# The sigmoid of the decay taken as a tangent, with its halving on GpSimd

## The chip, the cores and the metric

The kernel runs on one core of a Trainium2 chip. The metric is the device time of one execution in microseconds, the median of several runs. A core has TensorE (matmuls), VectorE, ScalarE (activation functions from a table, and copies), GpSimd and SyncE (which issues most of the transfers). In profiles they are PE, DVE, ACT, POOL and SP; PEld is TensorE's loading of weights.

## The reference

Two stages in a row. The first is a gated linear recurrence over 768 tokens for 4 batches and 8 heads of size 48; the second an MLP with a gelu over all 3072 tokens (384 to 2048 to 384).

```python
def _attn_ref(q, k, v, f_logit):                     # (4, 8, 768, 48) each
    f = 1.0 / (1.0 + np.exp(-f_logit))
    state = np.zeros((B, H, D, D))
    for t in range(S):
        state = f[:, :, t, :, None] * state + np.einsum('bhd,bhe->bhde', k[:, :, t], v[:, :, t])
        y[:, :, t] = np.einsum('bhd,bhde->bhe', q[:, :, t], state)

def _moe_ref(x, w_in, w_out):                        # x: y as (3072, 384)
    h = x @ w_in
    g = h * (1.0 / (1.0 + np.exp(-1.702 * h)))
    return g @ w_out
```

## The kernel before

The work is cut into 12 units of 256 tokens, numbered n, three to a batch. A unit n goes through an attention part and, later, its MLP.

Attention treats a unit as four chunks of 64 tokens. F holds the decay f of a unit as 128 x 1024 numbers in one buffer, since four pairs of heads times 256 tokens lie along it. From F, GpSimd makes products of neighbours over 1, 2, 4, ... 32 tokens (`begin_gates`, L383, tile tot, one buffer that is reused from unit to unit). With F and then with these products VectorE scales the keys and queries in X, level by level (`promote`, L473 in units 0 to 2 and L477 later). Ahead of each such step ScalarE sets the keys aside (Kc, L448, and Qc, L454), and TensorE takes the scores (sc, L392), which VectorE masks into A (L421, L441). The values v are summed by A (y, L488); the state st is carried over the chunks on VectorE (L594, L595), and adds its share to y (L616). ScalarE copies y to yT (L627), and transfers turn yT into xT, the input of the MLP.

The MLP multiplies xT by w_in (h, L785), applies the gelu on ScalarE (g, L789, the function Gelu_apprx_sigmoid), and multiplies g by w_out (o, L811 in blocks for units 0 to 2, L762 later, where seven products take the place of eight). The weights come in as 32-bit words, and are converted once, in units 0 to 4, by one ScalarE instruction (L217, tile a) and four of VectorE (L219 to L222).

How F comes about differs by unit. In units 0 to 2 (`n < N_FILL`, N_FILL is 3) TensorE transposes the raw logits (L344) into PSUM, and ScalarE evicts them with four activations of 128 x 256 (L349); in units 0 and 1 the function of this eviction is the sigmoid, in unit 2 it is a copy, and the sigmoid follows in one instruction on all of F (L355). From unit 3 on VectorE transposes the raw logits into F in two halves (L332), and one activation of 128 x 1024 applies the sigmoid in place (L337).

ScalarE takes its functions from a table that is loaded in sets; where the next function is not in the set that is loaded, the compiler puts a load ahead of it (ACT_TABLE_LOAD in the profile, at the line of the function that it is for). The sigmoid and the gelu lie in different sets.

The order on TensorE is written out by hand, and for units 0 to 3 that of all engines: `merge` runs through the parts of a unit's attention and puts matmuls of the MLP between them, with pieces of the weight conversion on VectorE and ScalarE. The parts that prepare unit n + 1 (`begin_f`, `begin`, `begin_k`, `begin_gates`) are placed among those of unit n. PSUM tiles for h, o and the transposes share one tag "mm" of four buffers, so TensorE cannot start the next h before ScalarE has emptied one of them.

Of the kernel before, what the change touches and what calls it, by code (L numbers as in the profile page):

```python
# [12 lines left out]
AF = mybir.ActivationFunctionType  # L13
ALU = mybir.AluOpType


def view(t, offset, dims):

    a = t[:]
    return bass.AP(a.tensor, a.offset + offset, [list(a.ap[0])] + [list(d) for d in dims])  # L20
# [3 lines left out]
def kernel(  # L24
# [33 lines left out]
    nc = tc.nc  # L58
# [18 lines left out]
    N_FILL = 3  # L77
    HALF = U // 2
    SLOT = NP * HALF
# [68 lines left out]
    F = const.tile([P, NA], F32, name="F")  # L148
# [21 lines left out]
    for r in range(NGR):  # L170
        ffs = range(r * FG, (r + 1) * FG)
        for ff in ffs[::2]:
            f = slice(ff * P, (ff + 2) * P)
# [65 lines left out]
    def load_raw(n, j, engines=(nc.sync,)):  # L239
        if n >= NALL:  # L240
            return
        b, s0 = n // NU, n % NU * U
        src = (f_logit, q, k)[j]
        first = s0 - (j == 1)

        def span(head, token, dims, d=0):
            return bass.AP(src.tensor, src.offset + ((b * H + head) * S + token) * D + d, dims)
        if n < N_FILL:
            for a in range(NP):
                engine = engines[a * len(engines) // NP]  # L250
                to = by_pair[j][32 * a:32 * (a + 1), :, :R * D]
                if first < 0 and a == 0:

                    for r, rows in ((1, 16), (17, 15)):
                        engine.dma_start(
                            out=to[r:r + rows], in_=span(0, r * R - 1, [[R * D, rows], [S * D, 2], [1, R * D]])
                        )
                    engine.dma_start(out=to[:1, :, D:], in_=span(0, 0, [[R * D, 1], [S * D, 2], [1, (R - 1) * D]]))
                else:
                    engine.dma_start(out=to, in_=span(2 * a, first, [[R * D, 32], [S * D, 2], [1, R * D]]))  # L260
            return
        for f in (1, 0):
            for r in range(4):
                lo = 32 * (r % 2)
                width = R4 * D - lo
                part = span(r // 2, first + (0 if f else HALF), [[R4 * D, 32], [2 * S * D, NP], [1, width]], lo)
                nc.sync.dma_start(out=by_half[32 * r:32 * (r + 1), j, f, :, :width], in_=part)
            if f and first < 0:
                for r in range(4):
                    lo = 32 * (r % 2)  # L270
                    nc.sync.dma_start(
                        out=by_half[32 * r:32 * r + 1, j, f, :, :D - lo],
                        in_=q[b - 1, r // 2::2, S - 1:S, lo:].rearrange("a t d -> t a d"),
                    )
# [31 lines left out]
    def attention(n):  # L306
# [8 lines left out]
        ORDER = (1, 0) if n % 2 == 0 else (0, 1)  # L315
# [10 lines left out]
        def turn(j, outs, fn=None):  # L326

            if n >= N_FILL:
                for f in (1, 0):
                    out = outs(f)  # L330
                    at, step = (0, 1) if f else (HALF - 1, -1)
                    nc.vector.transpose(  # L332
                        view(out, at, [[HALF, NP], [step, R4], [R4 * step, 32]]),
                        by_half[:, j, f].rearrange("p a (j d) -> p (a j) d", j=R4)[:, :, :32],
                    )
                if fn:
                    nc.scalar.activation(F, F, fn)  # L337
                return
            for j0 in range(0, R, 4):
                pt = ps.tile([P, 4, P], F32, tag="mm", name=f"t_{n}_{j}_{j0}", bufs=4)  # L340
                for jj in range(4):
                    for h in range(2):
                        x = (j0 + jj) * D
                        nc.tensor.matmul(  # L344
                            pt[h * HS:(h + 1) * HS, jj, :], lhsT=by_pair[j][:, h, x:x + HS], rhs=ident, start=True, stop=True
                        )
                for f in (1, 0):
                    at, step = (j0, 1) if f else (HALF - 1 - j0, -1)
                    nc.scalar.activation(  # L349
                        view(outs(f), at, [[HALF, NP], [R * step, 16], [step, 4]]),  # L350
                        pt.rearrange("p j (a f i) -> p f a i j", a=NP, f=2)[:, 1 - f],
                        fn if fn and n < N_FILL - 1 else AF.Copy,
                    )
            if fn and n == N_FILL - 1:
                nc.scalar.activation(F, F, fn)  # L355

        def begin_f():
            turn(0, lambda f: F[:, ORDER.index(f) * SLOT:(ORDER.index(f) + 1) * SLOT], AF.Sigmoid)
            if n >= N_FILL or (n == 1 and 0 == 0):
                load_raw(n + 1, 0)  # L360

        def begin():
            turn(1, lambda f: slot(query(n, f)))
            if n >= N_FILL or (n == 1 and 1 == 0):
                load_raw(n + 1, 1)

        def begin_k():
            turn(2, lambda f: slot((KR, KF)[f]))
            if n >= N_FILL or (n == 1 and 2 == 0):
                load_raw(n + 1, 2)  # L370
            if n >= N_FILL:
                set_aside(0, True)
                promote(0)
            else:
                set_aside(0)
# [268 lines left out]
        def to_x(y, x, ng):  # L644

            queue = nc.sync if n else nc.scalar
            for h in range(2):
# [3 lines left out]
                while at < D:  # L651
# [5 lines left out]
                    at += w  # L657

        return (begin_f, begin, begin_k, begin_gates), parts


# [353 lines left out]
```

## Time and profile before

Three runs took 627.27, 628.38 and 629.58 us; the median is 628.38 us. The profiled execution has a span of 627.9 us.

| engine | busy us | share of the span | instructions |
|---|---|---|---|
| TensorE, matmuls | 602.8 | 96% | 7314 |
| TensorE, weight loads | 517.5 | 82% | 7314 |
| VectorE | 385.8 | 61% | 632 |
| ScalarE | 260.3 | 41% | 544 |
| GpSimd | 39.9 | 6% | 91 |

The weight loads overlap the matmuls. ScalarE's busy time holds 20 table loads. In a line of the timeline the first number is the start in us, the second the length, then come engine, source line, operation, output and inputs, and in brackets the idle time before it with what ended it. In a line of the groups the numbers after the bar are the group's busy time in us, the mean of one instruction in ns, and the idle time ahead of it.

### The profile page before, as it was taken

What the parts mean: (1) busy time and instruction counts of PE and PEld (TensorE: products, weight loads), DVE (VectorE), ACT (ScalarE), POOL (GpSimd) and SP (SyncE); (2) the same over time, 40 slices, a digit from 0 to 9 for tenths busy, and PEclk for the clock granted to TensorE, in tenths of its full rate; (3) what the DMA queues carried; (4) which work ended last, traced back from release to release, by engine and by line L of the source; (5) the groups of instructions that cost most, each with busy time, mean ns of one, the idle gap of its engine ahead of it and who ended that gap; (6) DMA issues with size and microseconds to landing.
All of it is one profiled execution on the core that took longest, in us unless ns stands there. A gap on an engine that the chain in (4) does not pass through costs nothing.

```text
span 627.9 us, 17094 instructions
## 1 busy us (share of the span) xinstructions
PE 602.8 (96%) x7314; PEld 517.5 (82%) x7314; DVE 385.8 (61%) x632; ACT 260.3 (41%) x544; POOL 39.9 (6%) x91
## 2 busy tenths in 40 slices
PE   7958999889999999999999999999999999999997
PEld 5647776757678688989989989989989889889896
DVE  1778976575876755677566577656658645521441
ACT  3436543533244534543544454354354353233220
POOL 3010030020001001001001001001001001000000
PEclk9898999989999999999999999999999999999999
DMA  7646675652034444444452342552161121001000
GB/s 171 183 126 165 170 161 158 148 139 76 2 92 99 122 100 105 105 94 110 122 135 60 76 109 73 142 123 68 45 160 33 44 59 27 27 1 27 26 1 25
DMA packets 83308, 58.20 MB, mean 93 GB/s; under 512 B 33633, under 2 KB 75265, under 8 KB 83233
## 3 DMA queue, kind: packets, MB, share of 16 engines
q1 hardware_dynamic: 82192, 55.55, 35.4%
q10 hardware_dynamic: 1041, 1.57, 1.0%
q8 instruction: 57, 0.93, 0.7%
q14 instruction: 18, 0.15, 0.1%
HBM read 43.98 MB, written 8.39 MB: 83 GB/s over the span
## 4 chain that ended last, share of the span: by engine, by line
PE 87%; DVE 6%; ACT 3%; DMA 2%; issue 1%; SPq 1%; ACTq 0%; DVEq 0%
PE h L785 38%; PE o_X L762 8%; PE o_Y L762 8%; PE o L811 8%; PE o_Z L762 7%; PE sc L392 6%; PE o_W L762 4%; PE t L344 3%; PE y L616 2%; PE sc L576 2%; PE y L488 1%; PE idle L108 1%; DVE a L221 1%; DMA xT<-yT 1%; ACT yT L627 1%
## 5 line engine op out<-in xcount | busy, mean ns | idle before, releaser
L785 PE MATMUL h<-xT,w_in 128*128 128x256 f32 (+1 forms) x1152 | 257.4, 381 | 2.4 <-ACT g L789 1.9
L785 PEld LDWEIGHTS h<-xT,w_in 128*128 128x128 f32 x1152 | 216.4, 190 | 34.2 <-ACT g L789 2.1
L789 ACT ACTIVATE g<-h 128x256 f32<-128x256 f32 (+1 forms) x192 | 72.0, 383 | 156.8 <-PE h L785 156.5
L477 DVE TENSOR_TENSOR X<-X,tot 128x1024 f32<-128x1024 f32 x45 | 55.1, 1224 | 62.6 <-PE sc L392 49.4
L448 ACT COPY Kc<-X 128x512 f32<-128x512 f32 x72 | 48.0, 666 | 83.4 <-DVE X L477 51.3
L811 PE MATMUL o<-w_out,g 128*128 128x384 f32 x192 | 67.5, 501 | 3.0 <-DVE w_out L222 3.0
L811 PEld LDWEIGHTS o<-w_out,g 128*128 128x128 f32 x192 | 36.2, 194 | 26.0 <-DVE w_out L222 3.6
L762 PE MATMUL o_X<-w_out,g 128*128 128x192 f32 x288 | 52.6, 331 | 0.0
L762 PE MATMUL o_Y<-T,S 128*128 128x192 f32 x288 | 51.9, 329 | 0.0
L441 DVE COPY_PREDICATED A<-masks,sc 128x256 f32<-128x256 uint32 (+1 forms) x108 | 50.9, 534 | 0.1
L762 PEld LDWEIGHTS o_Y<-T,S 128*128 128x128 f32 x288 | 46.9, 190 | 1.5 <-issue 0.7
L762 PEld LDWEIGHTS o_X<-w_out,g 128*128 128x128 f32 x288 | 46.7, 190 | 1.0
L383 POOL TENSOR_TENSOR tot<-F 128x512 f32<-128x512 f32 x12 | 12.5, 1039 | 478.2 <-DVE st L594 429.3
L392 PE MATMUL sc<-X,Kc 48*64 48x64 f32 x1440 | 31.1, 224 | 10.7 <-ACT Kc L448 9.6
L392 PEld LDWEIGHTS sc<-X,Kc 48*64 48x64 f32 x1440 | 26.4, 138 | 18.0 <-ACT Kc L448 11.4
L332 DVE STREAM_TRANSPOSE X<-raw 128x512 f32<-128x512 f32 x36 | 37.9, 1101 | 2.9 <-PE y L616 2.8
L700 DVE TENSOR_TENSOR g<-g,g 128x512 f32<-128x512 f32 x18 | 12.5, 692 | 40.4 <-ACT g L789 40.4
L627 ACT COPY yT<-y 48x256 f32<-48x256 f32 x92 | 33.7, 366 | 7.8 <-PE y L616 5.3
L473 DVE TENSOR_TENSOR X<-X,tot 128x512 f32<-128x512 f32 x30 | 20.3, 688 | 13.1 <-PE sc L392 11.0
L383 POOL TENSOR_TENSOR tot<-tot 128x256 f32<-128x256 f32 (+4 forms) x60 | 24.6, 410 | 4.7
L762 PE MATMUL o_W<-T,g 128*128 128x192 f32 x144 | 24.9, 326 | 0.0
L762 PE MATMUL o_Z<-w_out,g 128*128 128x192 f32 x144 | 24.9, 326 | 0.0
(92 smaller groups left out, 629.1 us busy)
## 6 DMA issues: line engine op xcount, KB each, us to landing
bits<-in_moe_w_out_dram SPq DMA_DIRECT2D x8, 768.0 KB, 5.0
raw<-in_f_logit_dram SPq DMA_DIRECT2D x48, 96.0 KB, 2.3
raw<-in_k_dram SPq DMA_DIRECT2D x48, 96.0 KB, 2.3
raw<-in_q_dram SPq DMA_DIRECT2D x44, 96.0 KB, 2.3
bits<-in_moe_w_in_dram SPq DMA_DIRECT2D x7, 576.0 KB, 6.2
k_tok<-z SPq DMA_DIRECT2D x56, 64.0 KB, 1.8
kt<-k_tok SPq DMA_DIRECT2D x14, 256.0 KB, 2.8
out_dram<-osb SPq DMA_DIRECT2D x18, 192.0 KB, 1.8
```

Source lines behind the costliest of these rows:

```text
L332: nc.vector.transpose(view(out, at, [[HALF, NP], [step, R4], [R4 * step, 32]]), by_half[:, j, f].rearrange("p a (j d) -> p (a j) d", j=R4) ...
L383: nc.gpsimd.tensor_tensor(tn, t2[:, :, 0], t2[:, :, 1], ALU.mult)
L392: nc.tensor.matmul(t["sc"][g * HS:(g + 1) * HS, h, a, s, :], lhsT=t["Kc", l][rows(h), x:x + HS], rhs=rhs(h, a, g), start=True, stop=True,)
L441: nc.vector.copy_predicated(out=view(A, at, dims), mask=mask.bitcast(U32), data=got)
L448: nc.scalar.copy(c.rearrange("p (n two m) -> p n two m", two=2, m=m), view(X, KF * SLOT, [[2 * m, SLOT // (2 * m)], [(KR - KF) * SLOT + m, ...
L473: nc.vector.tensor_tensor(x, x, y, ALU.mult)
L477: nc.vector.tensor_tensor(x, x, y, ALU.mult)
L627: copy(view(yT[rows(h)], at, [[U, NP], [step, HS]]), py[columns(h, g), g, :, f, :])
L762: nc.tensor.matmul(t[bank], lhsT=lhs(f), rhs=rhs(f), start=(new and f == 0), stop=(f == HF - 1), skip_group_check=True,)
L785: nc.tensor.matmul(ph, lhsT=w_in[:, c, ff * P:(ff + 1) * P], rhs=xTs[n][:, c, :], start=(c == 0), stop=(c == NK - 1))
L789: nc.scalar.activation(g[ff // FG][:, ff % FG, :], ph, AF.Gelu_apprx_sigmoid)
L811: nc.tensor.matmul(t["po"], lhsT=g[ff // FG][:, ff % FG, tt * P:(tt + 1) * P], rhs=w_out[:, ff, :], start=(ff == ffs[0]), stop=(ff == ffs[ ...
```

## The change

The sigmoid is written as 0.5 + 0.5 tanh(x / 2). The tangent is in the same table set as the gelu, and in that of the sigmoid too, so ScalarE need not change its set for F. ScalarE applies the tangent with a scale of 0.5, and GpSimd then does the halving and the addition in place, in one instruction on the 128 x 1024 numbers of F. Unit 0 keeps the sigmoid, which the set loaded at the start has. In units 1 and 2 the tangent is applied in the eviction from PSUM; the separate sigmoid of unit 2 falls away. In units 3 to 11 the tangent takes the place of the sigmoid on all of F.

```diff
                 if fn:
-                    nc.scalar.activation(F, F, fn)
+                    fn()
                 return
...
-                        fn if fn and n < N_FILL - 1 else AF.Copy,
+                        (AF.Tanh if n else AF.Sigmoid) if fn else AF.Copy, scale=0.5 if fn and n else 1.0,
                     )
-            if fn and n == N_FILL - 1:
-                nc.scalar.activation(F, F, fn)
+            if fn and n:
+                half_up()
+
+        def half_up():
+            nc.gpsimd.tensor_scalar(F, F, 0.5, 0.5, op0=ALU.mult, op1=ALU.add)
+
+        def sigmoid():
+            nc.scalar.activation(F, F, AF.Tanh, scale=0.5)
+            half_up()
 
         def begin_f():
-            turn(0, lambda f: F[:, ORDER.index(f) * SLOT:(ORDER.index(f) + 1) * SLOT], AF.Sigmoid)
+            turn(0, lambda f: F[:, ORDER.index(f) * SLOT:(ORDER.index(f) + 1) * SLOT], sigmoid)
```

In the changed program ScalarE has 2 table loads in place of 20 and one activation fewer, and GpSimd has 11 instructions more, one ahead of each unit's tot chain from unit 1 on. Apart from one small transfer of q_end (L981), which moves back by one place, the order of the instructions on the other engines is the same.

## The prediction

> **What bounds the kernel now.** I read the busy times first, then the windows of 20 us over the whole span, then the waits of TensorE, and then the timeline where TensorE waits.
>
> ```profile
> PE 602.8 (96%) x7314; PEld 517.5 (82%) x7314; DVE 385.8 (61%) x632; ACT 260.3 (41%) x544; POOL 39.9 (6%) x91
> ```
>
> TensorE is busy for 602.8 of 627.9 us, so every gain that does not shorten TensorE's own work must come out of some 25 us of its idle time. The windows say where these lie (columns: PE, PEld, DVE, ACT and POOL busy, each with its count; the granted clock; DMA share; GB/s):
>
> ```profile
> 20.00:40.00 20.00, 17.89 (x462) 14.15 (x458) 16.97 (x34) 9.84 (x22) 1.34 (x2) 0.99 0.63 164
> 40.00:60.00 20.00, 12.01 (x155) 9.60 (x154) 16.43 (x29) 9.56 (x17) 1.47 (x5) 0.83 0.54 124
> 60.00:80.00 20.00, 19.32 (x392) 14.58 (x392) 18.92 (x32) 11.69 (x26) 1.43 (x2) 1.00 0.77 192
> 100.00:120.00 20.00, 18.55 (x131) 12.61 (x129) 12.81 (x21) 7.97 (x12) 0.00 (x0) 1.00 0.64 165
> 120.00:140.00 20.00, 16.45 (x295) 11.83 (x296) 12.18 (x19) 7.15 (x15) 4.19 (x6) 0.91 0.69 168
> 480.00:500.00 20.00, 20.00 (x255) 18.58 (x244) 13.96 (x24) 10.17 (x23) 0.00 (x0) 1.00 0.15 41
> ```
>
> From 260 to 620 us every window has TensorE at 20.00 of 20, as in the last line here. All waits lie in the first 150 us, but for 0.46 us at 240. In 60 to 80 us VectorE stands at 18.92 of 20: there it is as full as TensorE. The busy figure is not flattering itself: 84 matmuls of h in a row take 18.33 us in the chain of waits, 218 ns each, in unit after unit alike, where a hidden stall would scatter.
>
> The table loads that the change is aimed at:
>
> ```profile
> L789 ACT ACT_TABLE_LOAD x10 | 12.8, 1283 | 0.2
> L337 ACT ACT_TABLE_LOAD x9 | 11.5, 1283 | 19.7 <-DVE F L332 19.7
> L337 ACT ACTIVATE F<-F 128x1024 f32<-128x1024 f32 x9 | 9.5, 1060 | 0.1
> L355 ACT ACTIVATE F<-F 128x1024 f32<-128x1024 f32 x1 | 1.1, 1057 | 0.0
> ```
>
> Each sigmoid of units 3 to 11 has a load ahead of it, and the next gelu has one too. And the one place where TensorE waits for such a load:
>
> ```profile
> 115.53 1.28 ACT L337 ACT_TABLE_LOAD   x1
> 116.82 1.06 ACT L337 ACTIVATE F<-F 128x1024 f32<-128x1024 f32 x1
> 117.78 0.89 ACT L217 ACTIVATE a<-bits 128x768 f32<-128x768 f32 x1
> 118.69 1.28 ACT L789 ACT_TABLE_LOAD   x1
> 119.99 0.38 ACT L789 ACTIVATE g<-h 128x256 f32<-128x256 f32 x1
> 120.42 4.15 PE L785 MATMUL h<-xT,w_in 128*128 128x256 f32 x18 [1.87 <-ACT g L789]
> ```
>
> All four buffers of the tag "mm" are full; the gelu that frees one stands behind both loads, and TensorE is idle for 1.87 us.
>
> **What the Trainium skill says.** "ScalarE: Activation LUTs", section "What ACT_TABLE_LOAD costs", gives about 1283 ns for the load and about 1380 ns for a drain with it. The trace agrees on 1283 ns and shows no drain beside it (load at 115.53, its ACTIVATE at 116.82). "GPSIMD Engine Reference", section 3.1, puts a simple loop at 1.03 cycles an element; and its section 1 says that GpSimd shares SBUF interfaces with VectorE, in conflict with VectorE instructions that have two SBUF inputs or run in a two-port mode. The trace shows that conflict:
>
> ```profile
> 78.50 1.04 POOL L383 TENSOR_TENSOR tot<-F 128x512 f32<-128x512 f32 x1 [36.71 <-DVE st L594]
> 78.63 2.47 DVE L473 TENSOR_TENSOR X<-X,F 128x512 f32<-128x512 f32 x2
> ```
>
> Two such promotions take 1.28 us elsewhere. Here the pair takes 2.47, its first one 1452 ns (the longest in the list of F's readers) against a median of 693. The POOL instruction keeps its 1039 ns in all twelve cases, so it is VectorE that loses: 0.77 us within 1.04 us of POOL work.
>
> **The change part by part.**
>
> *Removed, table loads.* In the order of the changed program ScalarE has 2 loads in place of 20: one at the start, one ahead of the first gelu. That is 18 × 1.283 = 23.1 us of ScalarE. The 16 for units 4 to 11 lie where TensorE has no wait but the 0.46 us at 240, which is for a copy of kn with no load near it: worth nothing, hidden by TensorE's own work. The two of unit 3 (115.53 and 118.69) count. Without them F's activation is at 115.5 to 116.6, a's at 116.5 to 117.4, the gelu ends near 117.8, and TensorE, whose matmuls of tkn run to 118.55, finds a free buffer. It gains the whole 1.87 us and no more. I see nothing below to give it back: the next waits (129.3, for w_out on VectorE at the end of a chain that starts from TensorE's sc L576; 146.2, for xT) move with it, and their loads were issued long before.
>
> *Removed, the separate sigmoid of unit 2* (L355, 1.06 us at 52.78). It stands in the chain of waits ahead of Kc and of sc at 56.93. But VectorE works from 52 to 78 us almost without a break (1.1 us of gaps in 26 us, by the windows of 2 us), and the chain passes to it at 63: st at 78.36, then Kc, then sc at 82.47. TensorE waits for it there anyway. I count 0.1 us.
>
> *Added, 11 GpSimd operations on 128x1024 f32, in place.* No row has this one. From below: 1024 × 1.03 cycles at the page's 1.2 GHz = 0.88 us, an estimate from that page; POOL's 128x384 memset of 0.42 us scaled by size gives 1.11. From above: two inputs on 512 elements cost 1.04 us, so 2.1 us for 1024. I take 1.1 us, since there is one input. On POOL's own queue only the tot chain of the same unit stands behind it, and that waits for st L594: by the waits it sits idle 429.3 us in ten waits. F is ready at 116.6 in unit 3 and tot starts at 129.1; later units have more room. X<-X,F comes later still. So the wait for the halved F is free.
>
> What is not free is VectorE's loss beside it, in the two places where VectorE sets the pace. *Unit 1*: F is evicted at 28.0 us, the halving runs to 29.1 and meets L473 (two inputs, 0.69 us, start 27.98). It loses up to 0.7; some 0.2 of this is slack, since the second of the L473 at 29.74 waits for TensorE until 30.48. From there tkn, y, st, yT and the transfers of xT follow in one chain to sc at 47.88: 0.5 us. *Unit 2*: F is evicted at 52.75, the halving runs from 52.8 to 53.9 and meets L222 (two inputs, 52.99), then L473. At 0.77 lost per 1.04 us, 1.1 × 0.74 = 0.8 us, and VectorE is full until 78, so TensorE gets it. From unit 3 on the halving meets VectorE at 60 to 70% load with TensorE full: nothing.
>
> *Moved*: the evictions of F in units 1 and 2 take the tangent with a scale of 0.5 at the same size, 383 ns, no change; one small q_end transfer moves back a place in the SP queue, nobody waits for it.
>
> Sum: −1.87 − 0.1 + 0.5 + 0.8 = −0.7 us: 628.4 − 0.7 = 627.7.
>
> **The rivals.**
> 1. *No contention.* VectorE shows no loss, because one input leaves the shared interface idle half the time. For it: L441 right after in unit 1 reads PSUM. Against: the 1452 ns above. Then −1.87 − 0.1: 626.4.
> 2. *A slow halving; slower than before.* At 2.1 us and full contention: 2.1 × 0.74 = 1.55 in unit 2 and about 1.1 in unit 1, so −2.0 + 2.65 = +0.7: 629.1. For it: POOL's two-input rate. Against: one input.
> 3. *The loads are worth more.* If the lighter ScalarE also took the wait at 129.3 (2.96 us) and the half clock behind it (clock 0.50 in 134 to 136), 3 to 5 us more: about 623. "TensorE: Matmul & The Clock Gate", Part 1, ties the clock to a free-running window of 3.4 us of activity, so a stall moved by 1.9 us may fall otherwise in it; the trace agrees in so far as 2.96 us idle was followed by half clock and 1.87 us was not. Against: that wait hangs on VectorE and TensorE, not on ScalarE. All 23 us on the path (605) I rule out: TensorE is full.
> 4. *A new wait in the steady stage*, POOL against VectorE's X and Kc in each of nine units, 0.5 us each on top of the forecast: about 632. Against: no idle of TensorE there at all today, so there is slack.
>
> **How the numbers follow.** Forecast 0.45, rival 1 0.25, rival 2 0.18, rival 3 0.08, rival 4 0.04. The three runs of before span 627.3 to 629.6, so about 1 us of scatter goes on each side of the first three: 625.2 to 630.0. Faster by over 0.5% means below 625.2: rival 3 and the low edge of rival 1, 0.11. Slower by over 0.5% means above 631.5: rival 4, 0.04. The rest is 0.85.
>
> **What would show it.** Right: two loads on ScalarE, its busy time down by some 24 us; the wait of h for g at 118.5 gone; TensorE still at 20.00 of 20 from 260 us; L473 at 28 and L222 or L473 at 53 longer than 0.69 and 0.96 us; the new POOL rows at 1.0 to 1.3 us. Wrong: those two at their old durations (rival 1), POOL rows near 2 us (rival 2), a smaller stall at 129 (rival 3), or waits of TensorE past 260 us (rival 4).

## The result and the profile after

The changed kernel took 626.91 us (median of 20 runs, 625.27 to 628.89) against 628.88 us before (20 runs, 626.52 to 631.99): ratio 0.9965 of the means, 95% interval 0.995 to 0.9981. That is 2.2 us faster, between 1.2 and 3.1. Two repetitions on other occasions gave 0.9956 (0.994 to 0.9973) and 0.9973 (0.996 to 0.9986).

The busy times of the changed kernel, from its page:

```profile
PE 600.5 (96%) x7314; PEld 516.9 (83%) x7314; DVE 388.3 (62%) x632; ACT 237.3 (38%) x525; POOL 53.4 (9%) x102
```

ScalarE lost 23.0 us of work and the kernel 2.2: nine tenths of what was removed was never on the path. GpSimd has 13.5 us more. The groups of F's new instructions, and the loads that are left:

```profile
L359 POOL TENSOR_SCALAR F<-F 128x1024 f32<-128x1024 f32 x11 | 13.6, 1233 | 112.1 <-ACT F L362 87.9 <-ACT F L349 24.2
L362 ACT ACTIVATE F<-F 128x1024 f32<-128x1024 f32 x9 | 9.5, 1056 | 19.6 <-POOL tot L391 19.6
L112 ACT ACT_TABLE_LOAD x1 | 1.3, 1283 | 0.7 <-PEq L1007 0.7
L797 ACT ACT_TABLE_LOAD x1 | 1.3, 1283 | 0.0
```

A mean of 1233 ns hides two kinds of halving, undisturbed and drawn out. The list of F's instructions has the spread (minimum, median, maximum):

```profile
L359 POOL TENSOR_SCALAR F<-F x11: 1048/1084/1747, 26.3 to 475.8; 128x1024 f32<-128x1024 f32 x11
```

Undisturbed it takes 1.05 us, as priced; the longest, 1.75 us, is that of unit 2. The place of the old stall, in the timeline of the changed kernel (ScalarE's and TensorE's lines):

```profile
114.57 1.05 ACT L362 ACTIVATE F<-F 128x1024 f32<-128x1024 f32 x1
115.52 0.95 ACT L217 ACTIVATE a<-bits 128x768 f32<-128x768 f32 x1
116.32 0.42 ACT L797 ACTIVATE g<-h 128x256 f32<-128x256 f32 x1
...
117.12 0.60 PE L540 MATMUL tkn<-ident,X 128*128 128x128 f32 x4
117.55 4.05 PE L793 MATMUL h<-xT,w_in 128*128 128x256 f32 x18
```

The gelu runs right behind F's and a's activations, and h follows the transposes of tkn with no gap. The windows of 20 us say the same (PE busy first):

```profile
100.00:120.00 20.00, 20.00 (x140) 14.20 (x139) 14.14 (x22) 7.17 (x14) 1.05 (x1) 1.00 0.64 174
480.00:500.00 20.00, 20.00 (x225) 18.35 (x224) 14.03 (x23) 6.07 (x15) 0.00 (x0) 1.00 0.19 54
```

### The profile page after: what moved, and what is told of

Same layout as the page of the kernel before. It is cut to its first block, busy times and chain, and to the rows that moved or that the text cites. A ratio compares the mean times of both kernels' runs of the same rounds, so it can differ in the third digit from the quotient of the medians.

```text
span 624.7 us, 17089 instructions
## 1 busy us (share of the span) xinstructions
PE 600.5 (96%) x7314; PEld 516.9 (83%) x7314; DVE 388.3 (62%) x632; ACT 237.3 (38%) x525; POOL 53.4 (9%) x102
## 4 chain that ended last, share of the span: by engine, by line
PE 87%; DVE 7%; ACT 2%; issue 1%; DMA 1%; SPq 0%; DVEq 0%; ACTq 0%
PE h L793 38%; PE o_X L770 8%; PE o_Y L770 8%; PE o L819 8%; PE o_Z L770 7%; PE sc L400 6%; PE o_W L770 4%; PE t L344 2%; PE y L624 2%; PE sc L584 2%; PE y L496 2%; ACT yT L635 1%; DVE X L481 1%; DVE a L221 1%; PE idle L108 1%
## 5 line engine op out<-in xcount | busy, mean ns | idle before, releaser
L449 DVE COPY_PREDICATED A<-masks,sc 128x256 f32<-128x256 uint32 (+1 forms) x108 | 50.9, 535 | 0.1
L332 DVE STREAM_TRANSPOSE X<-raw 128x512 f32<-128x512 f32 x36 | 37.9, 1102 | 3.0 <-PE y L624 2.9
L481 DVE TENSOR_TENSOR X<-X,tot 128x512 f32<-128x512 f32 x30 | 21.1, 717 | 11.9 <-PE sc L400 11.1
```

The source lines that it names most:

```text
L332: nc.vector.transpose(view(out, at, [[HALF, NP], [step, R4], [R4 * step, 32]]), by_half[:, j, f].rearrange("p a (j d) -> p (a j) d", j=R4) ...
L449: nc.vector.copy_predicated(out=view(A, at, dims), mask=mask.bitcast(U32), data=got)
L481: nc.vector.tensor_tensor(x, x, y, ALU.mult)
```

## The experiments

Two executions of one program differ by a few us in their first 50 us already, through clock and transfers, so I compare stretches inside the traces, each between two points that the same engine passes:

- stretch V, where VectorE sets the pace: from the start of the w_out conversion (L222) near 52 us to the start of the last y of unit 1 near 77 us
- stretch S, round the old stall: from that y to the o that waits for w_out near 130 us

```
kernel        V us    S us    ratio to before (95%)
before        25.00   54.30
changed       25.70   52.16   0.9965 (0.995 to 0.9981)
early_only    25.71   54.30   0.9995 (0.9978 to 1.0012)
late_only     24.86   52.16   0.9943 (0.9921 to 0.9966)
dose_u2       27.38   52.15   0.9978 (0.9967 to 0.999)
dose_u1       25.59   52.14   0.9974 (0.996 to 0.9988)
u3_only       24.87   52.15   0.9942 (0.9921 to 0.9962)
u4_on         25.79   56.00   0.9997 (0.998 to 1.0015)
dose_late     25.71   52.14   0.9965 (0.9951 to 0.9978)
after_again   25.73   52.15   0.9956 (0.994 to 0.9973)
no_355        25.55   56.00   1.0001 (0.9983 to 1.0019)
late_again    24.86   52.13   0.995 (0.9934 to 0.9966)
after_third   25.69   52.13   0.9973 (0.996 to 0.9986)
```

The kernels are described one by one below; `after_again` and `after_third` are the changed kernel on other occasions. What follows S, from that o to the end of the program, takes 495.3 to 495.6 us in eleven of the thirteen traces, with the 16 loads of units 4 to 11 and without them. The two exceptions (`after_again` 496.3, `dose_u1` 497.8) have a longer stretch at half clock near 135 us.

V is long in `u4_on` and `no_355` although they have no halving in unit 2. There VectorE waits 0.84 and 0.60 us for an sc that came late, since TensorE ran the matmuls ahead of it at half clock, until 51.9 and 52.3 us. Without that wait V is 24.95 in both. In `dose_late` the half clock lasted until 52.8, and V is 25.71 all the same: the wait and the loss to the halving seem to overlap in such an execution, so the halving of unit 2 costs its full price only in the others.

After both traces gave V +0.70 and S −2.14, I had theory A: the halving of unit 2 costs what the forecast said, and the stall was worth more than its 1.87 us. Its rival B: VectorE's loss is absorbed and the loads are worth 2 us.

**Which half of the change does it.** `late_only` keeps the plain sigmoid in the evictions of units 0 to 2, where its set is still loaded:

```diff
-                        (AF.Tanh if n else AF.Sigmoid) if fn else AF.Copy, scale=0.5 if fn and n else 1.0,
+                        AF.Sigmoid if fn else AF.Copy,
...
-            if fn and n:
-                half_up()
```

> Units 0 to 2 take the plain sigmoid in the eviction from PSUM (that set is still loaded then), with no halving and no separate sigmoid; units 3 to 11 have tangent and halving as in the changed kernel; 2 table loads. Theory A (the halvings of units 1 and 2 cost VectorE time that TensorE gets, about 0.4 and 0.85 us, and the loads of unit 3 are worth more than the 1.87 us of the stall): about 1.2 us faster than the changed kernel, so 3.2 to 3.5 us below before, ratio 0.9945 to 0.995. Theory B (those halvings are absorbed, the loads are worth 2 us): the same as the changed kernel, ratio 0.9965 to 0.997.

`early_only` keeps units 1 and 2 as in the change and gives units 3 to 11 the old sigmoid:

```diff
         def sigmoid():
-            nc.scalar.activation(F, F, AF.Tanh, scale=0.5)
-            half_up()
+            nc.scalar.activation(F, F, AF.Sigmoid)
```

> Units 1 and 2 as in the changed kernel (tangent in the eviction, halving on GpSimd, no separate sigmoid in unit 2), units 3 to 11 with the sigmoid and its table loads as before: 20 loads. Theory A: 1.2 us slower than before, ratio 1.002, with the pair of L481 beside the halving of unit 2 at about 2.1 us in place of 1.28, and the stall of h for g of 1.87 us near 119 still there. Theory B: ratio 0.9995 to 1.000.

`late_only` is the lowest of this set, 0.9943; in V it has 24.86 us, 0.84 less than the changed kernel. `early_only` has the changed kernel's V and the old S, stall included. Its time, 0.9995, does not fit the 1.2 us that theory A had for the two halvings together (1.002, where the interval ends at 1.0012). The 0.7 us by which its V is longer would be 1.0011, still inside. So the time favours B, the stretches favour A at a smaller size, and the doses had to decide.

**What one halving costs, by dose.** Three more operations on F of the same size, which change nothing in its values:

```diff
             nc.gpsimd.tensor_scalar(F, F, 0.5, 0.5, op0=ALU.mult, op1=ALU.add)
+            for _ in range(3 if n == 2 else 0):
+                nc.gpsimd.tensor_scalar(F, F, 1.0, 0.0, op0=ALU.mult, op1=ALU.add)
```

> The changed kernel with three more GpSimd operations of the same size on F in unit 2 (times 1, plus 0). Theory A: each costs VectorE about 0.8 us near 52 to 59 us and TensorE gets it from 75 us on, so up to 2.5 us above the changed kernel, ratio to before about 1.000; the st of unit 1 (L602, at 74.7 in the changed kernel) is later by 2 to 2.5 us against the start of sc at 46.3. Theory B: ratio stays at 0.9965.

The same with `n == 1`:

> The changed kernel with three more GpSimd operations of the same size on F in unit 1 (times 1, plus 0). Theory A: VectorE loses up to 0.7 us to each near 26 to 33 us, some of it in its waits for TensorE, and yT follows: 1 to 2 us above the changed kernel, ratio to before 0.998 to 1.000. Theory B: ratio stays at 0.9965.

In unit 2 the three lengthen V by 1.68 us, 0.56 each, less than the 0.8 that I had set; the ratio rises from 0.9965 to 0.9978, which is less (0.8 us), but the two intervals leave room for 1.7. So the loss reaches TensorE, whose y ends V, but in the dose GpSimd takes a part of it itself: its three took 1.05 to 1.36 us each. Both ratios lie below what theory A had expected of the doses (1.000 here, 0.998 to 1.000 for unit 1, where 0.9974 was measured). In unit 1 I compare from the sc near 21 us to the last y of unit 0, less one wait of TensorE near 29 us that the profile puts down to issue (0 to 1.5 us, in kernels with and without a halving alike; its cause stays open). That is 15.94 us in the changed kernel and in `dose_late`, with the halving, and 15.94 in `late_only`, `u3_only` and `u4_on`, without it; 16.36 in `dose_u1`. One halving in unit 1 costs nothing, three more cost 0.4 us.

Why the two units differ shows in the timeline. Unit 1 in the changed kernel, VectorE's lines and GpSimd's:

```profile
26.16 0.69 DVE L481 TENSOR_TENSOR X<-X,tot 128x512 f32<-128x512 f32 x1 [0.58 <-PE sc L400]
26.26 1.52 POOL L359 TENSOR_SCALAR F<-F 128x1024 f32<-128x1024 f32 x1 [13.98 <-ACT F L349]
26.77 0.77 DVE L449 COPY_PREDICATED A<-masks,sc 128x256 f32<-128x256 uint32 x2
```

VectorE's L481 with two SBUF inputs was under way first and keeps its 0.69 us; GpSimd gets 1.52 in place of 1.05. The L449 that come next read PSUM and lose nothing beside it. Unit 2 in the changed kernel:

```profile
51.43 0.96 DVE L222 TENSOR_TENSOR w_out<-a,s 128x768 f32<-128x768 f32 x1
51.55 1.75 POOL L359 TENSOR_SCALAR F<-F 128x1024 f32<-128x1024 f32 x1 [10.21 <-ACT F L349]
52.31 2.13 DVE L481 TENSOR_TENSOR X<-X,tot 128x512 f32<-128x512 f32 x2
```

GpSimd ends 0.9 us after L222 does (53.30 and 52.39), as if it had waited for it, and the pair of L481 behind it pays: 2.13 in place of 1.28. In `after_again` F was ready just before L222, and the roles were changed over:

```profile
52.02 1.04 POOL L359 TENSOR_SCALAR F<-F 128x1024 f32<-128x1024 f32 x1 [10.81 <-DVE a L221]
52.03 1.84 DVE L222 TENSOR_TENSOR w_out<-a,s 128x768 f32<-128x768 f32 x1
53.79 1.28 DVE L481 TENSOR_TENSOR X<-X,tot 128x512 f32<-128x512 f32 x2
```

The halving keeps its 1.04 us, L222 takes 1.84 in place of 0.96. Either way VectorE loses 0.85 to 0.88.

**Which loads count.** On `late_only`, the tangent in unit 3 alone, or in units 4 to 11 alone (the test turned round):

```diff
         def sigmoid():
+            if n > N_FILL:
+                nc.scalar.activation(F, F, AF.Sigmoid)
+                return
             nc.scalar.activation(F, F, AF.Tanh, scale=0.5)
             half_up()
```

> Units 0 to 2 with the plain sigmoid in the eviction and no halving; unit 3 alone with tangent and halving; units 4 to 11 with the sigmoid and both loads as before: 18 loads in place of 20. Theory A (all the gain is the stall of unit 3 near 119, 2.1 us in the traces, plus the half clock that follows it in a part of the executions): 2.3 to 3.3 us below before, ratio 0.995 to 0.9965, and no wait of h for g near 118. Theory C (the 16 loads of units 4 to 11 are worth something too): less than that, ratio 0.997 or more.

> The complement: units 0 to 2 with the plain sigmoid in the eviction and no halving, unit 3 with the sigmoid and its two loads, units 4 to 11 with tangent and halving: 4 loads. Theory A: 0.1 us below before, ratio 0.999 to 1.0005, the stall of 1.87 us near 119 still there, TensorE full from 260 us on. Theory C: 1 us or more below before, ratio 0.9985 or less.

`u3_only` removes 2 loads of 20 and has the whole gain, 0.9942. That is 3.6 us, more than the 2.3 to 3.3 expected, though the interval (0.9921 to 0.9962) reaches into that range. `u4_on` removes 16 loads and gains nothing, 0.9997. Its interval leaves room for 1.3 us, but in the traces what follows S is only 0.3 us shorter than before (495.3 and 495.6). The 16 loads of the steady stage, 20.5 us of ScalarE, are worth nothing that can be measured.

`u4_on` had a surprise in S: 56.00 us, 1.7 more than before. Its windows of 4 us (clock behind the POOL column), and below those of before:

```profile
116.00:120.00 4.00, 2.13 (x12) 1.69 (x11) 2.36 (x4) 3.97 (x7) 0.00 (x0) 1.00 0.82 209
120.00:124.00 4.00, 4.00 (x13) 3.21 (x12) 0.90 (x2) 0.99 (x4) 0.00 (x0) 0.57 0.86 174
```

```profile
116.00:120.00 4.00, 2.55 (x16) 2.03 (x14) 1.26 (x3) 3.96 (x5) 0.00 (x0) 1.00 0.70 168
120.00:124.00 4.00, 3.58 (x17) 3.16 (x18) 2.01 (x3) 2.38 (x6) 0.00 (x0) 1.00 1.00 240
```

The stall is the same 1.87 us in both; in `u4_on` 3.4 us of half clock follow it (120.1 to 123.5). Four traces have the stall: before and `early_only` without the half clock (S 54.30), `u4_on` and `no_355` with it (S 56.00). Every kernel without the stall has S at 52.13 to 52.16. So the stall cost 2.14 us in each of the four, and another 1.7 us, 3.84 together, in two of them.

What sets these two apart can be read from the traces. In all thirteen the half clock comes in pieces of 3.41 us, or in two or three such pieces on end, and within a trace the pieces begin whole multiples of 3.41 us apart (in `u4_on` at 38.2, 45.0, 120.1 and 133.8). So each trace can be divided into stretches of 3.41 us, and where they begin differs from execution to execution. In `u4_on` and `no_355` the whole stall lies inside one stretch (116.72 to 120.13 and 117.17 to 120.59), of which TensorE works 1.54 and 1.55 us, and the next stretch has the half clock. In before and `early_only` the end of a stretch (119.56 and 119.01) cuts the stall in two, TensorE works 1.9 us or more of each stretch, and the full clock stays. If this is what decides, the chance for a stall of 1.87 us to fall into one stretch is (3.41 − 1.87) / 3.41 = 0.45, an estimate. Idle time alone does not decide: in `dose_u1` a stretch with 1.98 us of it (from 125.4) was followed by full clock. Four traces make a pattern, not a rule.

**The steady stage under load.** The dose with `n >= N_FILL`, 27 operations more:

> The changed kernel with three more GpSimd operations of the same size on F in each of the units 3 to 11 (27 in all, some 28 us of GpSimd). Theory A (TensorE hides all of it there): the same as the changed kernel, ratio to before 0.9965, no wait of TensorE past 260 us. Rival (VectorE is slowed and TensorE waits for it): 0.8 us in each of nine units, 7 us, ratio about 1.008.

0.9965, the changed kernel's own ratio. GpSimd spent 37.7 us on the 27, and TensorE never waited past 260 us:

```profile
300.00:400.00 100.00, 100.00 (x1292) 92.02 (x1291) 68.72 (x106) 40.09 (x88) 16.42 (x20) 1.00 0.41 101
400.00:500.00 100.00, 100.00 (x1282) 91.28 (x1281) 66.65 (x102) 39.06 (x87) 16.63 (x20) 1.00 0.33 83
```

**The separate sigmoid of unit 2.** The kernel before, with one edit:

```diff
-                        fn if fn and n < N_FILL - 1 else AF.Copy,
+                        fn if fn else AF.Copy,
...
-            if fn and n == N_FILL - 1:
-                nc.scalar.activation(F, F, fn)
```

> The kernel before, with the sigmoid of unit 2 applied in the eviction and so without the separate activation on all of F; nothing else changed, all 20 loads, no tangent. Theory A (VectorE sets the pace of this stretch): 0.1 us below before, ratio 0.999 to 1.001; from the w_out conversion on VectorE near 52 us to the last y of unit 1 near 77 us 24.9 us in place of 25.0. Rival (the activation stands on the path, as the chain of waits says): 1.06 us below before, ratio 0.9983.

1.0001: no gain seen, though the interval ends at the rival's 0.9983. The trace is closer to a verdict. V is 25.55 us, and 24.95 without the 0.60 us wait for the late sc. In `late_only` and `u3_only`, which lack the activation too, V is 24.86. The separate sigmoid is worth some 0.1 us, as VectorE sets the pace.

**The better version.** `late_only` again, beside the changed kernel:

> The version without the halvings of units 1 and 2 once more, beside the changed kernel on the same chip. By the traces it should be 0.85 us below the changed kernel (the VectorE time that the halving of unit 2 takes), so 2.3 to 3.3 us below before, ratio 0.9945 to 0.9965. If the halving of unit 2 costs nothing in time, the two are equal.

> The changed kernel on the chip of late_again. Ratio to before 0.9955 to 0.9975, 0.85 us above late_again.

> The changed kernel once more, on the same chip as its variants. Ratio 0.9965; its span from the sc after the long wait near 46 us to the last y of unit 1 near 77 us is longer by 0.8 us than in the variants without halving in unit 2.

`late_again` took 625.89 us, `after_third` 627.12, before 629.09. The change without its halvings in units 1 and 2 is thus 1.2 us below the change as made, at 0.995 of before (0.9934 to 0.9966, against 0.996 to 0.9986). With it, `late_only` and `u3_only` (0.9943 and 0.9942) lie below all three measurements of the changed kernel (0.9956 to 0.9973). `u3_only` is the same but for 16 loads that cost nothing. The version without the early halvings is thus faster than the kernel before in every measurement. Against the changed kernel the intervals still overlap a little, but V has the same sign, 24.86 us against 25.69.

## Why the prediction was right, and where it was off

The forecast said 0.7 us faster, with a range of 625.2 to 630.0 us. Measured were 2.2 us, three times the forecast, inside that range. What gains and what loses was named rightly, but two terms of the sum were off, and both made the gain too small: the stall was priced too low, and the halving in unit 1 was charged to VectorE, which lost nothing.

- *Loads of the steady stage, nothing*: right, shown by `u4_on`. TensorE at 20.00 of 20 in every window was the line to trust.
- *Loads of unit 3, −1.87 us, "the whole 1.87 us and no more"*: too small. S shortens by 2.14 us: 2.01 up to the h that had waited (77.99 to 120.42 before, 77.13 to 117.55 after), whose first matmuls now overlap the end of tkn, and 0.13 from there to the o. And the half clock after the stall, which I had seen not to follow in the one trace of before, does follow in others, at 1.7 us. If that happens half the time (two traces of four, and 0.45 by the estimate above), it is 0.85 us on the mean.
- *Separate sigmoid, −0.1*: right, some 0.1, though it stood in the chain of waits at its full 1.06 us.
- *Halving in unit 1, +0.5*: wrong, 0. My step "it is VectorE that loses" took one collision, in which the GpSimd instruction had started first, for a rule. Here VectorE's had: L481, the old L473, keeps its 0.69 us. The forecast's own times had it so, with L473 starting at 27.98 and the eviction of F ending at 28.0.
- *Halving in unit 2, +0.8*: right, 0.85, with the mechanism and the path (VectorE full until 78 us) as said.
- *Price of the halving, 1.1 us*: right, 1.05 where nothing disturbs it, up to 1.75 beside VectorE. The wait for F was free, as said.

With the measured sizes: −2.14 − 0.14 + 0.85 = −1.4 us in executions where the clock held, and −0.85 more for the half clock's share: −2.3, against −2.2 measured. This last term is an estimate, and the interval of the measurement, 1.2 to 3.1 us, holds the 1.4 as well. It is supported by the times: every kernel without the stall came out faster than its V and S say. The changed kernel gained 2.2, 2.8 and 1.7 us for 1.4, and `late_only`, `late_again` and `u3_only` gained 3.6, 3.1 and 3.6 us for 2.3. But `early_only`, which keeps the stall, also came out 1 us faster than its V says (−0.3 for +0.7 us), so this is support and no proof. The mean clock of whole executions cannot settle it: it is 0.988 to 0.991 with the stall and without it, and six of the nine traces without the stall have one more piece of half clock after TensorE's last matmul, where it costs nothing.

Of the rivals, the first (no contention, −2.0) came nearest in time for a wrong reason: contention is there, 0.85 us. The second fell on the length of the halving, the fourth on `dose_late`. The third named the clock, but at the wrong stall. The wait for w_out near 129 us stays 2.9 us long, and one piece of half clock behind it costs nothing that the rest of the program shows (two pieces, in `after_again` and `dose_u1`, went with 0.8 us and 2.3 us more). In `dose_u2` it did not come,

```profile
130.49 3.49 PE L821 MATMUL o<-w_out,g 128*128 128x384 f32 x10 [2.94 <-DVE w_out L222]
135.89 1.11 PE L626 MATMUL y<-X,st 48*48 48x64 f32 x64 [1.91 <-DVE X L487]
```

and in the changed kernel it did:

```profile
129.29 4.93 PE L819 MATMUL o<-w_out,g 128*128 128x384 f32 x10 [2.94 <-DVE w_out L222]
134.69 1.11 PE L624 MATMUL y<-X,st 48*48 48x64 f32 x64 [0.48 <-DVE X L485]
```

From o to y are 5.40 us in both, because y waits for VectorE's X. "TensorE: Matmul & The Clock Gate", Part 1, says that the window in which activity is counted runs free of the kernel; that fits the stretches of 3.41 us above, which begin elsewhere in each trace, and a stall of equal length being followed by half clock in some executions and not in others.

## What to carry to other kernels

Removing work from an engine that does not set the pace is worth only the waits in which it held up the one that does: find these first, here one stall of 1.87 us behind 2 loads of 20. Price a stall of TensorE with the half clock that may follow it, and do not read its absence from a single trace. When work goes to GpSimd, look at what VectorE has in flight at that moment, and leave the work out where VectorE is full, as `late_only` does.

## What was not expected of the hardware

GpSimd and VectorE do not share evenly in a collision. Beside VectorE's instructions with two SBUF inputs, whichever came first kept its time, and the other was longer by nearly what was left of it: the halving 1.52 and 1.75 us in place of 1.05, L222 1.84 in place of 0.96, a pair of L481 2.13 in place of 1.28. L449, which reads one input from PSUM, ran beside the halving at its usual 0.77 us for two. L332, a transpose with a single SBUF input, took 1.14 to 1.15 us beside it in units 7, 9 and 11, little more than its usual 1.10. One input is no safeguard, though: L220, an integer operation on 128x768 numbers with one input, took 1.27 us in place of 0.56 beside an added operation in `dose_late`.

A stall of 1.87 us was enough for 3.41 us at half clock, in the two traces of four in which it lay inside one of the stretches of 3.41 us.
